# The opening of a retention + ELU kernel: second chunk first, two scalings on another engine, fewer blank products

## The chip, the cores and the metric

The kernel runs on one core of a Trainium2 chip. The metric is the device time of one execution in microseconds (us); the figure for a kernel is the median of several executions. The engines work in parallel, each through its own queue in order, and wait for each other on semaphores: TensorE (PE, with its weight loads PEld), VectorE (DVE), ScalarE (ACT), GpSimd (POOL), and SyncE (SP), whose queue starts all transfers here.

## The reference

Two blocks follow each other. A retention layer, as a recurrence over 768 tokens for 4 batches and 8 heads of 64:

```
for t in range(S):
    state = gamma * state + k[t] (outer) v[t]
    y[t]  = scale * q[t] @ state
```

with gamma = 1 - 2^(-5-h) for head h. Its output, as 3072 tokens of 512 values, goes through two matrix products with an ELU between:

```
h = x @ w_in                       # 512 -> 2048
g = where(h > 0, h, exp(min(h, 0)) - 1)
out = g @ w_out                    # 2048 -> 512
```

Everything is computed in float32. The weights come as 64-bit floats, and the kernel narrows them on the chip.

## The kernel before

The retention works in chunks of 128 tokens; four chunks are a block of 512 tokens (six blocks). For a chunk, the kernel scales v by powers of gamma (`scale_v`), forms scores of q and k within 64-token halves (`score_products`), masks them (`mask_pair`, `scores`), forms the outer products of k and v for the states (`state_products`) and adds them up (`state_sum`). The outputs are sums of two products in PSUM, one within a half (`within`) and one across halves with the state (`across`); VectorE multiplies them by a table of powers (`etab`, built by `powers_of` on ScalarE) into `xb`, the input of the first matrix product. Ahead of the second half of the "across" products, a tiny VectorE copy into `seen` reads PSUM, so that PE waits for the first half.

The weights arrive in sixteen pieces of 1 MB (`wraw`). `prepare` has ScalarE take a piece apart in two or three operations, in one or two halves; with `by_vector` VectorE does the third. `decode` is a generator: each `take()` lets VectorE do the next step, a shift (L191) or a merge (L194, which writes `w_a` or `w_b`), and when a piece is exhausted the next load is issued, which waits until its buffer is free. Pieces 0 and 2 go to `w_a`, pieces 1 and 3 to `w_b`.

The first block's first matrix product is done plainly, in sixteen tiles (`plain_first`); later blocks use Strassen's scheme of seven products. Because only 256 tokens are ready at first, the first five tiles are computed in two halves of columns, and the very first tile begins with a quarter, 128 tokens, as soon as chunk 0 has gone through.

The order of the work is written out by hand: instructions enter each engine's queue in the order in which the program text issues them[...]. The opening (from the function `unread` on) is a list of calls that interleaves chunk 0, chunk 1, the pieces 0 to 2, chunks 2 and 3, and the first five tiles. Two things there feed nothing: `unread(count, n)` multiplies a blank tile into a PSUM bank that nobody reads, and a loop does the same with 28 small blank products ahead of the first scores. They keep PE at work.

The transfers of the opening are issued in this order: chunk 0 in two halves (q and k first), half of piece 0, chunk 1, the other half of piece 0, piece 1, chunk 2, chunk 3, piece 2. The scaling of chunks 0 and 1 runs on VectorE, that of all others on GpSimd (L281):

```
eng = nc.vector if m < 2 else nc.gpsimd
```

Of the kernel before, what the change touches and what calls it, by code (L numbers as in the profile page):

```python
# [18 lines left out]
def kernel(  # L19
# [32 lines left out]
    nc = tc.nc  # L52
# [3 lines left out]
    B, H, S, D, DM, DFF = dims  # L56
    NTOK = B * S
    C = P
    TB = 512
    TH = TB // 2  # L60
# [69 lines left out]
    def load_piece_parts(parts, behind=None):  # L130
        n = len(staged)
        if n < NPIECE:

            t = stage.tile([P, 1024, 2], U32, name="wraw", tag="stage")
            hold(t[:, :, 0].bitcast(FP32), behind)
            staged.append(t)
            for part in range(parts):
                if part:
                    yield
                c = slice(part * 1024 // parts, (part + 1) * 1024 // parts)  # L140
                d = slice(2 * c.start, 2 * c.stop)
                nc.sync.dma_start(t[:, c].rearrange("p c w -> p (c w)"), w_bits[n].bitcast(U32)[:, d])
# [1 line left out]

    def prepare(parts=1, by_vector=False, between=None):

        n = len(prepared)
        if n >= NPIECE:  # L150
            return
        t = staged[n]
        if n < 2 * NQ:
            dst = (w_a, w_b)[n % 2][n // 2].rearrange("p a b c d -> p (a b c d)")
        else:

            dst = w_s[n % NQ].rearrange("p a b c d -> p (a b c d)")[:, 0:1024]
        todo = []
        for part in range(parts):
            if part and between:  # L160
                between()
            c = slice(part * 1024 // parts, (part + 1) * 1024 // parts)
            lo, hi, flat = t[:, c, 0], t[:, c, 1], dst.bitcast(U32)[:, c]
            nc.scalar.activation(flat, lo, AF.Copy, scale=2.0**-29)
            top = dst.bitcast(F8).rearrange("p (c b) -> p c b", b=4)[:, c, 3]
            nc.scalar.activation(top, hi.bitcast(FP32), AF.Copy, scale=2.0**-120, saturate=False)
            if not by_vector:
                nc.scalar.activation(lo.bitcast(FP32), hi.bitcast(FP32), AF.Copy, scale=2.0**-112)
            todo.append((lo, flat, hi if by_vector else None))
        prepared.append((dst, todo))  # L170
# [75 lines left out]
    def powers_of(tokens):  # L246
        for a in range(2):
            for u in range(2):
                nc.scalar.activation(etab[:, a, u, tokens], post[:, tokens], AF.Exp, scale=lny[:, a, u : u + 1])
# [4 lines left out]
    parts = load_piece_parts(2)  # L254
# [17 lines left out]
    carry = [const.tile([P, HP, D], FP32, name=f"carry{n}") for n in range(2)]  # L272
    held = {}

    def scale_v(m):
        if m >= NCHUNK:
            return
        i = chunks[m][1]
        qk, kv = raw[m]
        eng = nc.vector if m < 2 else nc.gpsimd  # L280
        eng.tensor_tensor(  # L281
            out=kv[:, 1], in0=kv[:, 1], in1=vf[:, i].unsqueeze(2).to_broadcast([C, H, D]), op=ALU.mult
        )
# [18 lines left out]
    def score_products(sc, tb, pp, x):  # L302
        qk = raw[tb * CPB + 2 * pp + x][0]
        for p in range(HP):
            for sub in range(2):
                for a in range(2):
                    nc.tensor.matmul(
                        sc[a][rows(sub), x, p, :], lhsT=qk[rows(a), 1, p, rows(sub)],
                        rhs=qk[rows(a), 0, p, rows(sub)], start=True, stop=True, skip_group_check=True,
                    )  # L310
# [13 lines left out]
    def mask_pair(sc, x):  # L324

        place = raw[x][0][:, 1].rearrange("p h c -> p (h c)").rearrange("p (a n t) -> p a n t", a=2, t=D)
        for a in range(2):
            nc.vector.tensor_tensor(
                out=place[:, a], in0=sc[a][:, x], in1=cmask.unsqueeze(1).to_broadcast([P, HP, D]), op=ALU.mult
            )  # L330
# [12 lines left out]
    def state_sum(kvs, tb, pp, x, sub, copy=None):  # L343
        n = 4 * pp + 2 * x + sub
        if fresh(tb, n + 1):
            return
        if fresh(tb, n):
            (copy or nc.scalar.copy)(state(tb, n + 1), kvs[sub][:, x])
        else:
            nc.vector.tensor_tensor(out=state(tb, n + 1), in0=kvs[sub][:, x], in1=state(tb, n), op=ALU.add)  # L350
# [117 lines left out]
    def flush():  # L468
        while later:
            later.pop(0)()  # L470

    def elu(g, h, depth=1, then=None):


        r = epool.tile([P, 512], FP32, name="r", tag="r", bufs=3)
        e = r if len(h.shape) == 2 else r.rearrange("p (a c) -> p a c", c=P)
        nc.scalar.activation(e, h, AF.Relu, scale=-1.0)  # L477
        nc.scalar.activation(e, e, AF.Exp, scale=-1.0)  # L478

        def last():  # L480
            nc.vector.scalar_tensor_tensor(g, e, -1.0, h, ALU.add, ALU.max)  # L481
            if then:
                then()

        while len(later) >= depth:
            later.pop(0)()
        later.append(last)

    def plain_first():

        tiles = [(n, w, row, fi) for n in range(NQ) for w, row in ((w_a, 0), (w_b, 1)) for fi in range(2)]
        banks = []

        def part(k, columns):
            n, w, row, fi = tiles[k]
            for j in range(4):
                nc.tensor.matmul(
                    banks[k][:, columns], lhsT=w[n][:, fi, j // 2, j % 2, :], rhs=xb[:, j, columns],
                    start=(j == 0), stop=(j == 3), skip_group_check=True,
                )  # L500

        for k in range(5):
            hp = bank("aabd"[k]) if k < 4 else ps_r.tile([P, 2, TH], FP32, name="hp", tag="r")
            banks.append(hp.rearrange("p a b -> p (a b)"))
            if k == 0:
                part(0, slice(0, C))
                yield
                part(0, slice(C, 2 * C))
            else:
                part(k, half[0])  # L510
            if k:
                yield
        for k in range(5):
            part(k, half[1])
            n, w, row, fi = tiles[k]
            elu(g_plain[row * NF + 2 * n + fi], banks[k])
            yield
        for k, (n, w, row, fi) in enumerate(tiles[5:]):
            hp = bank("aabd"[k % 4]).rearrange("p a b -> p (a b)")
            for j in range(4):  # L520
                nc.tensor.matmul(  # L521
                    hp, lhsT=w[n][:, fi, j // 2, j % 2, :], rhs=xb[:, j, :], start=(j == 0), stop=(j == 3)
                )
            elu(g_plain[row * NF + 2 * n + fi], hp)
            yield
        flush()
# [158 lines left out]
    def bank(x):  # L685
        return ps_f.tile([P, 2, TH], FP32, name="p" + x, tag=x, bufs=2 if x == "a" else 1)
# [409 lines left out]
    def take(count=1):  # L1096
        for _ in range(count):
            next(piece, None)
# [3 lines left out]
    def unread(count, n):  # L1102
        for _ in range(count):
            nc.tensor.matmul(warm[:, 0:n], lhsT=blank[:, 0:P], rhs=blank[:, 0:n], start=True, stop=True, skip_group_check=True)

    unread(1, TB)
    for n in range(28):
        nc.tensor.matmul(
            (warm, other)[n % 2][rows(n // 2 % 2), 0:D], lhsT=blank[rows(n % 2), 0:D], rhs=blank[rows(n % 2), 0:D],
            start=True, stop=True, skip_group_check=True,  # L1110
        )
# [8 lines left out]
    y = outputs_of_first()  # L1120
    next(y)
    next(y)
    unread(1, TB)
    score_products(sc, 0, 0, 1)
    state_sum(kvs, 0, 0, 0, 1)
    prepare(2, between=lambda: powers_of(slice(2 * C, S)))
    piece = decode(True)
    take()
    take()
    scale_v(1)  # L1130
    mask_pair(sc, 1)
    inner = plain_first()
    next(inner)
    state_products(kvs, 0, 0, 1, range(2))
    state_sum(kvs, 0, 0, 1, 0)
    next(y)
    next(y)
    next(y)
    unread(1, TB)
    next(y, None)  # L1140
    take()
    take()
    take()
    state_sum(kvs, 0, 0, 1, 1)
    scale_v(2)
    scale_v(3)
    prepare(2, by_vector=True)
    next(inner)
    piece = decode()
    take()  # L1150
    take()
    next(inner)
    scores(0, 1)
    states(0, 1)
    take()
    prepare(2)
    piece = decode(True)
    take()
# [26 lines left out]
    for n, _ in enumerate(inner):  # L1185
# [8 lines left out]
        elif n == 10:  # L1194
            scores(1, 0)
            scores(1, 1)
            parts = sums_of_pieces(0)
# [21 lines left out]
    for n in second_of_first():  # L1219
        send_small()  # L1220
        if n == 0:
            run(inputs_of_first(4, [xslot(x) for x in range(3)]))
            parts = sums_of_pieces(2)
# [8 lines left out]
        elif n == 2:  # L1232
            next_piece()
            parts = sums_of_pieces(4)
# [5 lines left out]
        elif n == 4:  # L1240
            run(inputs_of_first(6, [hslot(), hslot(), xslot(0)]))
            decode_all()
            parts = sums_of_pieces(6)
# [85 lines left out]
    for tb in range(2, NTB):  # L1329
# [24 lines left out]
        tail, parts = iter(()), combine_x_parts()  # L1354
# [122 lines left out]
```

## Time and profile before

| what | us |
|---|---|
| median of three executions | 635.99 |
| lowest, highest | 635.6, 638.48 |
| the profiled execution, its own time | 636.29 |
| span of its profile | 634.4 |
| PE busy in the span | 626.7 |
| PE busy in 0 to 7.9 / 7.9 to 30.6 | 6.45 / 20.91 |
| start of the second column half of the first tile (pa L497) | 30.56 |

The span is the time from the first to the last instruction in the profile; times in the timeline count from its start. A timeline row gives start and length in us, the engine, the line, the operation, what it writes and reads, shapes and the number of merged instructions; in brackets stands how long the engine was idle before and who released it. A float32 product on PE is recorded as two passes, so four products of 128x256 show as eight. The records of consecutive instructions overlap a little, so that a stretch of equal instructions is shorter than their lengths added up.

### The profile page before, as it was taken

How to read it: one execution, taken by the hardware profiler on the slowest of the kernel's cores; microseconds unless marked ns; L12 is line 12 of the kernel's file. 1: busy time of each engine (PE TensorE's matmuls, PEld its weight loads, DVE VectorE, ACT ScalarE, POOL GpSimd, SP SyncE). 2: the span in 40 equal slices, each digit the busy share in tenths (PEclk: the TensorE clock that was granted, in tenths of full speed). 3: DMA queues.
4: the chain of work that ended last, by engine and by line, in shares of the span. 5: the costliest groups of instructions: out<-in, count | busy, mean ns of one | idle time of the engine just before them, and what ended most of it. 6: DMA issues, size and time to landing. Idle time of an engine off the chain costs nothing.

```text
span 634.4 us, 16149 instructions
## 1 busy us (share of the span) xinstructions
PE 626.7 (99%) x6680; PEld 560.7 (88%) x6680; DVE 481.7 (76%) x870; ACT 252.9 (40%) x472; POOL 40.6 (6%) x40
## 2 busy tenths in 40 slices
PE   8999999999999999999999999999999999999998
PEld 5764568888899999889999989999988999988997
DVE  5779979978879685589676598867489878558975
ACT  6599635014551113554112556111465311366311
POOL 1111000003600000200000100000110000000000
PEclk9999999999999999999999999999999999999999
DMA  8698867687477778504889701789820697700794
GB/s 336 264 390 307 269 205 222 189 248 258 176 239 228 242 254 272 239 2 135 277 267 312 290 4 55 258 283 286 302 100 4 218 299 236 238 24 2 231 309 158
DMA packets 75897, 136.85 MB, mean 216 GB/s; under 512 B 6320, under 2 KB 31792, under 8 KB 70704
## 3 DMA queue, kind: packets, MB, share of 16 engines
q1 hardware_dynamic: 75824, 135.82, 64.2%
q8 instruction: 53, 0.87, 0.5%
q14 instruction: 20, 0.16, 0.1%
HBM read 114.56 MB, written 21.23 MB: 214 GB/s over the span
## 4 chain that ended last, share of the span: by engine, by line
PE 94%; DVE 4%; issue 1%; ACT 0%; DVEq 0%
PE pa L953 20%; PE pa L911 10%; PE pd L953 10%; PE pb L953 5%; PE pa L865 5%; PE pb L911 4%; PE pa L521 3%; PE qa L911 3%; PE x L611 3%; PE pa L740 2%; PE pd L865 2%; PE qd L911 2%; PE pd L911 2%; PE pa L611 2%; PE y L394 2%; PE kv L338 2%
## 5 line engine op out<-in xcount | busy, mean ns | idle before, releaser
L961 ACT COPY ms<-pa 128x128 f32<-128x128 f32 x104 | 27.6, 265 | 147.1 <-PE pa L953 143.7
L953 PE MATMUL pa<-ts,wq 128*128 128x128 f32 x560 | 74.2, 275 | 0.0
L953 PE MATMUL pd<-ts,wq 128*128 128x128 f32 x552 | 73.6, 276 | 0.1
L953 PEld LDWEIGHTS pa<-ts,wq 128*128 128x128 f32 x560 | 68.5, 192 | 0.4
L953 PEld LDWEIGHTS pd<-ts,wq 128*128 128x128 f32 x552 | 67.1, 192 | 0.9 <-DVE res L965 0.5
L953 PE MATMUL pa<-gC,wq 128*128 128x128 f32 x480 | 64.6, 278 | 0.0
L478 ACT ACTIVATE r<-r 128x512 f32<-128x512 f32 x96 | 60.5, 631 | 3.0
L953 PEld LDWEIGHTS pa<-gC,wq 128*128 128x128 f32 x480 | 59.0, 192 | 1.3
L477 ACT ACTIVATE r<-gC 128x512 f32<-128x512 f32 x64 | 39.9, 624 | 32.0 <-DVE gC L919 32.0
L965 DVE TENSOR_TENSOR res<-pd,ms 128x128 f32<-128x128 f32 x68 | 19.4, 286 | 39.6 <-PE pd L953 38.4
L281 POOL TENSOR_TENSOR chunk<-chunk,vf 128x512 f32<-128x512 f32 x22 | 26.3, 1199 | 318.4 <-DMA chunk<-in_qkv_dram 153.5
L481 DVE SCALAR_TENSOR_TENSOR gC<-r,gC 128x512 f32<-128x512 f32 x64 | 44.3, 724 | 0.7 <-ACT r L478 0.7
L827 DVE TENSOR_TENSOR ts<-gC,ts 128x512 f32<-128x512 f32 x60 | 41.3, 688 | 1.0
L827 DVE TENSOR_TENSOR ts<-gC 128x512 f32<-128x512 f32 x60 | 40.9, 682 | 0.0
L953 PE MATMUL pb<-gC,wq 128*128 128x128 f32 x240 | 31.7, 275 | 0.0
L986 ACT COPY res<-pa 128x128 f32<-128x128 f32 x34 | 9.0, 265 | 55.1 <-PE pa L953 55.1
L953 PEld LDWEIGHTS pb<-gC,wq 128*128 128x128 f32 x240 | 29.2, 192 | 0.0
L690 ACT COPY m<-pa 128x512 f32<-128x512 f32 x24 | 13.9, 581 | 30.1 <-PE pa L911 14.2
L919 DVE TENSOR_TENSOR gC<-qa,gC 128x512 f32<-128x512 f32 x8 | 5.5, 692 | 25.1 <-PE qa L911 18.3
L911 PE MATMUL pa<-xt,w_s 128*128 128x256 f32 x96 | 23.0, 382 | 0.0
L911 PE MATMUL pa<-xt,w_b 128*128 128x256 f32 x96 | 23.0, 382 | 0.0
L965 DVE TENSOR_TENSOR res<-res 128x512 f32<-128x512 f32 (+1 forms) x31 | 20.6, 666 | 3.0 <-DVE res L965 0.5
(256 smaller groups left out, 1258.4 us busy)
## 6 DMA issues: line engine op xcount, KB each, us to landing
wq<-scratch_dram SPq DMA_DIRECT2D x277, 256.0 KB, 4.2
chunk<-in_qkv_dram SPq DMA_DIRECT2D x23, 1024.0 KB, 8.3
wraw<-in_w_dram SPq DMA_DIRECT2D x15, 1024.0 KB, 6.1
out_dram<-res SPq DMA_DIRECT2D x14, 256.0 KB, 3.8
scratch_dram<-gT SPq DMA_DIRECT2D x12, 256.0 KB, 4.2
scratch_dram<-m SPq DMA_DIRECT2D x12, 192.0 KB, 5.6
scratch_dram<-so SPq DMA_DIRECT2D x4, 512.0 KB, 4.8
scratch_dram<-wi SPq DMA_DIRECT2D x2, 1024.0 KB, 5.1
```

Of the source, the lines that this page charges most:

```text
L281: eng.tensor_tensor(out=kv[:, 1], in0=kv[:, 1], in1=vf[:, i].unsqueeze(2).to_broadcast([C, H, D]), op=ALU.mult)
L477: nc.scalar.activation(e, h, AF.Relu, scale=-1.0)
L478: nc.scalar.activation(e, e, AF.Exp, scale=-1.0)
L481: nc.vector.scalar_tensor_tensor(g, e, -1.0, h, ALU.add, ALU.max)
L521: nc.tensor.matmul(hp, lhsT=w[n][:, fi, j // 2, j % 2, :], rhs=xb[:, j, :], start=(j == 0), stop=(j == 3))
L611: nc.tensor.matmul(X[j][:, d, :], lhsT=w[j][:, d * P : d * P + P], rhs=x[j], start=(n == 0 and d == 0), stop=at_end, skip_group_check=True,)
L827: sub = lambda o, x, y: nc.vector.tensor_tensor(out=o, in0=x, in1=y, op=ALU.subtract)
L865: nc.tensor.matmul(ps[:, f, :], lhsT=lhs[f], rhs=xs[j][k], start=(begin and f == 0), stop=True, skip_group_check=True,)
L911: nc.tensor.matmul(ps[:, fi, :], lhsT=w[:, fi, j2, :], rhs=x[:, j2, :], start=(j in (1, 7) and fi == 0 and j2 == 0), stop=(j2 == 1), skip_ ...
L953: nc.tensor.matmul(ps, lhsT=w[:, f, :], rhs=ts[j][k][:, f, :], start=(begin and f == 0), stop=(f == 3), skip_group_check=True,)
L961: nc.scalar.copy(m, ps)
L965: nc.vector.tensor_tensor(out=o, in0=x, in1=y, op=ALU.add)
```

## The change

The second chunk's score products, scaling, masks, state products and outputs come directly behind the first chunk's, and the first decode steps and the first quarter tile follow behind or between them. The powers for the tokens from 256 on are built behind piece 1's preparation, where they had stood between the halves of piece 0 (so `prepare` loses its `between`). The scaling of chunks 2 and 3 goes from GpSimd to VectorE, behind the decode of piece 1. The fourth tile's first half is itself split into two quarters, with the scores and states of chunks 2 and 3 between them. Of the blank products, 20 small ones remain of 28; the large one ahead of chunk 1's scores has 256 columns in place of 512; the one behind chunk 1's outputs is gone.

```diff
-    def prepare(parts=1, by_vector=False, between=None):
+    def prepare(parts=1, by_vector=False):
...
-            if part and between:
-                between()
...
-    def scale_v(m):
+    def scale_v(m, by_vector=False):
...
-        eng = nc.vector if m < 2 else nc.gpsimd
+        eng = nc.vector if by_vector or m < 2 else nc.gpsimd
...
                 part(0, slice(C, 2 * C))
+            elif k == 3:
+                part(k, slice(0, C))
+                yield
+                part(k, slice(C, 2 * C))
             else:
                 part(k, half[0])
...
-    for n in range(28):
+    for n in range(20):
...
     next(y)
     next(y)
-    unread(1, TB)
+    unread(1, TH)
     score_products(sc, 0, 0, 1)
     state_sum(kvs, 0, 0, 0, 1)
-    prepare(2, between=lambda: powers_of(slice(2 * C, S)))
+    prepare(2)
     piece = decode(True)
-    take()
-    take()
     scale_v(1)
     mask_pair(sc, 1)
-    inner = plain_first()
-    next(inner)
     state_products(kvs, 0, 0, 1, range(2))
     state_sum(kvs, 0, 0, 1, 0)
     next(y)
+    take()
     next(y)
+    take()
     next(y)
-    unread(1, TB)
+    inner = plain_first()
+    next(inner)
     next(y, None)
     take()
     take()
     take()
     state_sum(kvs, 0, 0, 1, 1)
-    scale_v(2)
-    scale_v(3)
     prepare(2, by_vector=True)
+    powers_of(slice(2 * C, S))
     next(inner)
     piece = decode()
     take()
     take()
+    take()
+    scale_v(2, True)
+    scale_v(3, True)
+    next(inner)
     next(inner)
     scores(0, 1)
     states(0, 1)
-    take()
     prepare(2)
     piece = decode(True)
     take()
```

## The prediction

> **What bounds the kernel now.** I read the page's shares and slices first, then the busy time in three stretches, then the timeline of each engine over the first 35 us, then the waits.
>
> ```profile
> PE 626.7 (99%) x6680; PEld 560.7 (88%) x6680; DVE 481.7 (76%) x870; ACT 252.9 (40%) x472; POOL 40.6 (6%) x40
> PE   8999999999999999999999999999999999999998
> ```
>
> TensorE is busy nearly everywhere. The stretches (PE busy is the second figure, then PEld, DVE, ACT, POOL) show where it is not:
>
> ```profile
> 0.00:7.90 7.90, 6.45 (x120) 4.18 (x124) 3.75 (x26) 3.23 (x6) 1.56 (x8) 1.00 0.78 255
> 7.90:30.60 22.70, 20.91 (x501) 16.19 (x494) 16.96 (x38) 16.38 (x23) 2.31 (x3) 1.00 0.82 330
> 30.60:634.40 603.80, 599.38 (x6073) 540.31 (x6071) 461.03 (x807) 233.27 (x443) 36.69 (x29) 1.00 0.64 211
> ```
>
> From 30.6 us on PE misses 4.4 us of 604 us: it sets the end, so the kernel ends earlier by what this stage starts earlier. The stage begins with the second halves of the first five products (pa L497 at 30.56). All that the change touches lies before it, where blank products, waits and real work alternate. The timeline there (start, length, then idle time before and its releaser):
>
> ```profile
> 5.00 1.08 PE L307 MATMUL sc<-chunk 64*64 64x64 f32 x32
> 10.81 0.69 PE L307 MATMUL sc<-chunk 64*64 64x64 f32 x32
> 11.83 1.13 PE L497 MATMUL pa<-xb,w_a 128*128 128x128 f32 x8 [0.33 <-DVE w_a L194]
> 16.16 3.11 PE L497 MATMUL pa<-xb,w_a 128*128 128x128 f32 x16
> 19.79 1.99 PE L497 MATMUL pb<-xb,w_b 128*128 128x256 f32 x8 [0.52 <-DVE w_b L194]
> 25.66 1.36 PE L394 MATMUL y<-chunk 64*64 64x64 f32 x63
> 27.81 0.69 PE L409 MATMUL y<-chunk 64*64 64x64 f32 x32 [0.26 <-DVE seen L378]
> 28.50 2.22 PE L497 MATMUL hp<-xb,w_a 128*128 128x256 f32 x8
> 30.56 3.62 PE L497 MATMUL pa<-xb,w_a 128*128 128x256 f32 x16
> ```
> ```profile
> 18.43 1.31 DVE L194 CUSTOM_DVE_ANT_0 w_b<-wraw,w_b 128x1024 uint16<-128x1024 uint16 x1
> 20.67 1.31 DVE L194 CUSTOM_DVE_ANT_0 w_b<-wraw,w_b 128x1024 uint16<-128x1024 uint16 x1
> 27.51 0.25 DVE L378 COPY seen<-y 128x8 f32<-128x8 f32 x2 [1.18 <-PE y L409]
> 28.57 1.29 DVE L384 TENSOR_TENSOR xb<-y,etab 128x512 f32<-128x512 f32 x2 [0.22 <-PE y L409]
> 18.12 1.07 POOL L281 TENSOR_TENSOR chunk<-chunk,vf 128x512 f32<-128x512 f32 x1 [3.05 <-DMA chunk<-in_qkv_dram]
> 20.37 1.06 POOL L281 TENSOR_TENSOR chunk<-chunk,vf 128x512 f32<-128x512 f32 x1 [1.18 <-DMA chunk<-in_qkv_dram]
> 22.86 0.69 ACT L164 ACTIVATE w_a<-wraw 128x512 uint32<-128x512 uint32 x1 [5.17 <-DMA wraw<-in_w_dram]
> 24.24 0.65 ACT L168 ACTIVATE wraw<-wraw 128x512 f32<-128x512 f32 x1
> 32.48 0.60 ACT L477 ACTIVATE r<-pa 128x512 f32<-128x512 f32 x1 [2.26 <-PE pa L497]
> ```
>
> The order to follow is y L394, seen L378, second half of y L409, hp, pa. ScalarE waited 2.26 us for PE at 32.48; VectorE's chain through the four merges (L194) of pieces 0 and 1 decides when PE gets to y.
>
> [...] there is a slow start: the 32 score passes took 1.08 us at 5.00 and 0.69 at 10.81. [...] the two w_b merges, begun inside the two GpSimd scalings, took 1.31 us, the other merges of this shape 0.68 to 0.69. [...]
>
> **The change, part by part.** Prices are from the timeline: a 128x256 pass 0.216 us, so four products (eight passes) 1.73 and with 128 columns 0.86; VectorE start to start 0.60 for a scaling, 0.34 for a sum, 0.45 + 0.60 for a shift and its merge.
>
> *Eight blank products fewer.* 56 passes filled 3.45 to about 5.0, so eight products are 0.43 us. The first chunk's q and k land at about 4.7 (issue at 0.74 plus 4.0, the shortest landing that the transfers show), so the scores start about 0.15 earlier, not 0.43. This 0.15 is lost again at the second chunk, which lands at about 10.5 by the transfer records.
>
> *Blank product before the second scores halved, a later one removed.* 0.43 and 0.86 us of PE. The scores of chunk 1 go from 10.80 to about 10.6, bound by the landing.
>
> *Chunk 1 first.* The shift and merge of piece 0's first half (L191 10.54, L194 10.99 to 11.68) and the first product (PE 11.83 to 12.89) no longer stand before chunk 1's scaling, masks and state products. New VectorE starts: scaling 10.57, masks 11.33 (scores end at 11.29), state sum 12.03, shift 12.37, the two "seen" copies 12.92, merge 13.08 to 13.77, xb 13.75 and 14.09, shift 14.43 (ScalarE is done with that half at 14.41, as before), merge 14.89 to 15.58, sum 15.49, then piece 1: 15.83, 16.28, merge 16.73 to 17.42. Before, piece 1's first merge ended at 19.74.
>
> *Scaling of chunks 2 and 3 to VectorE.* Adds 2 x 0.68 us to VectorE, removes 2.13 us of GpSimd and with it 2 x 0.62 us of blocked merge. Piece 1's second merge ends at 18.92 (before: 21.98). Then chunk 2's scaling 18.83, chunk 3's waits for its landing until 20.37 and ends at 21.05. Queued behind it stand the masks L318 and the state sums; PE waits for these, but chunk 3's scores are not done before 21.2, so this wait costs nothing. Without that cover it would cost up to 1 us.
>
> *Powers of the last tokens (4 x 0.64 = 2.55 us of ScalarE) moved behind piece 1.* Before they filled 9.92 to 12.47, ahead of a piece half that lands only about then. Now they fill 17.7 to 20.2, in the 5.17 us that ScalarE idles before 22.86. First use is L384, later than 26. Cost nothing; 2.55 us of ScalarE were the cover gone.
>
> *Fourth product split.* Its first 128 columns (0.86) before the scores of chunks 2 and 3, the rest behind their state products. The passes sum to the same; up to 0.2 for extra changes of shape.
>
> PE then: first product 13.92 and 14.78, second 15.73 (its weights: 15.58 + 0.15), third 17.57, fourth's first half 19.30, scores 20.2 to 21.25, states 22.2, fourth's rest to 23.1, y L394 at 23.1 (before 25.66). By the old distance (25.66 to 27.51) "seen" would come at 24.95. It can't: in VectorE's queue the shift of piece 2's first half stands ahead of it, and that needs ScalarE, which ends at 24.24 + 0.65 = 24.89 on a piece that lands at 22.8. No load ahead of that one is issued differently: SP's first eight issues keep their order and waits, and what comes free earlier (buffers of pieces 0 and 1) queues behind transfers that run anyway. So the shift starts at 24.93 and "seen" at 25.28. From there the old distances hold: y's second half +0.30, pa L497 +3.05, so pa at 28.33 instead of 30.56. **Gain: 27.51 - 25.28 = 2.23 us.** PE has about 0.3 us to spare against that floor.
>
> Behind it, ScalarE is free at 30.2 (third operation on piece 3, 29.09 + 1.14), and the first elu needs pa's product at about 30.2: 2.26 us earlier, just enough. The load of piece 5 waits on piece 2's last merge and moves from 30.92 to about 28.7, behind transfers that end by 28.1. The later loads follow their merges.
>
> The profiled execution had 636.29 us, 634.4 of span and 1.9 around it. Minus 2.2 it gives 634.1; it stood 0.3 above the median of 635.99, so I predict **633.8 us**.
>
> **Rivals.** (1) *Part only.* If the w_b merges are slow for another reason than GpSimd, they end 0.6 and 1.2 us later, the fourth product's first half starts at 20.55, y L394 at 24.4, "seen" at 26.2: gain 1.3, 634.7 us. The same follows if PE's small products take longer than their old distances. For it: only 0.3 us spare. Against: both long merges, and only these, lie on GpSimd operations.
> (2) *Swallowed.* ScalarE is 92 to 98% busy from 33 to 63; if it can't start earlier, PE runs into full PSUM banks and the gain is 0, 636.0. Against: its 2.26 us of waiting at 32.48, and one wait of 4.5 us for PE in the stretch to 80.
> (3) *Slower.* Less blank work leaves PE idle for some 0.4 us around 4.6 and more later[...]. Passes at half rate cost as much again: 0.39 for scores of a chunk, about as much for its states, 0.5 + 0.4 for its y, 0.86 for each 128-column quarter of the first product; from 7.9 to about 15 us that is some 3 us. [...] when the full rate comes only after the first product, at about 16, the gain is used up, and beyond, to about 20, it is 638. [...] Against: PE stays busy from 13.9 on and has no gap over 0.5 us before.
> (4) *More.* Piece 2's landing is a floor for everything here; over 2.5 us would need a stall behind 30.6 to vanish too: 633.0.
>
> **How the numbers follow.** Full gain (2.0 to 2.5) 0.58, part (0.6 to 2.0) 0.24, swallowed 0.07, slower 0.05, more 0.06. The likeliest gives 633.5 to 634.0. Parts and repetitions (635.6 to 636.3 but for one of 638.48) stretch the range to 632.8 to 636.0. A half per cent (3.2 us), about what a measurement of this kernel can tell from no change, is below 632.8 or above 639.2: faster 0.06, slower 0.03, same 0.91.
>
> **What would show it.** Right: sc of chunk 1 near 10.6; first product near 13.9; w_b merges of 0.69; pb L497 near 17.6; ScalarE still at 22.86; "seen" of y near 25.3, pa's second half near 28.3, first elu near 30.2, the rest shifted by the same 2.2. Wrong: score passes over 1 us at 10.6 (clock), an idle wait for chunk 3 that ends behind its scores, "seen" released by PE later than 25.5, or waits of PE for gC after 40 us.

## The result: slower by 0.4%

The changed kernel took 639.27 us in the median (637.21 to 642.23, 20 executions); the kernel before, beside it, 636.45 (635.25 to 639.21). The ratio is 1.0042, with a 95% interval of 1.003 to 1.0055: 2.7 us slower. The prediction was 633.8 us, a gain of 2.2, with a range that ended at 636.0: the change goes the other way. The profiled execution took 637.8 us with a span of 635.7, near the low end of the twenty, so the profile can account for about half of the loss only; the other half is taken up below.

The page of the changed kernel, its shares, slices and a queue of transfers that the page calls "instruction" (packets, MB, share of the transfer engines):

```profile
PE 624.2 (98%) x6670; PEld 560.0 (88%) x6670; DVE 482.1 (76%) x872; ACT 252.8 (40%) x472; POOL 37.6 (6%) x38
PE   7899999999999999999999999999999999999998
q8 instruction: 53, 0.87, 0.5%
```

The busy time in the same three stretches as before, the second one now ending where the second half of the first tile starts (31.8 instead of 30.6):

```profile
0.00:7.90 7.90, 6.01 (x136) 3.80 (x140) 3.92 (x27) 3.23 (x6) 1.56 (x8) 1.00 0.80 254
7.90:31.80 23.90, 18.67 (x479) 15.79 (x470) 16.49 (x40) 16.38 (x23) 0.17 (x1) 1.00 0.76 314
31.80:635.70 603.90, 599.49 (x6073) 540.43 (x6071) 461.64 (x807) 233.18 (x443) 35.88 (x29) 1.00 0.64 211
```

PE is busy for 2.24 us less in the second stretch than before (18.67 against 20.91; 1.3 of it is blank work taken out), and yet the stretch is 1.2 us longer: PE stands still there for 5.23 us instead of 1.79. The third stretch is as long as before, 603.9 against 603.8. So in the profile the whole difference is made in the opening. PE's timeline there:

```profile
10.62 0.69 PE L305 MATMUL sc<-chunk 64*64 64x64 f32 x32 [0.61 <-DMA chunk<-in_qkv_dram]
11.34 0.69 PE L336 MATMUL kv<-chunk 64*64 64x64 f32 x32
13.27 0.27 PE L392 MATMUL pb<-chunk 64*64 64x64 f32 x2 [1.16 <-issue]
15.20 3.77 PE L495 MATMUL pa<-xb,w_a 128*128 128x128 f32 x24 [0.23 <-DVE w_a L192]
18.96 1.97 PE L495 MATMUL pb<-xb,w_b 128*128 128x256 f32 x8
20.76 1.05 PE L495 MATMUL pd<-xb,w_b 128*128 128x128 f32 x8
21.75 1.16 PE L305 MATMUL sc<-chunk 64*64 64x64 f32 x64
23.77 1.16 PE L495 MATMUL pd<-xb,w_b 128*128 128x128 f32 x8
24.86 0.46 PE L392 MATMUL y<-chunk 64*64 64x64 f32 x15
27.56 0.93 PE L392 MATMUL y<-chunk 64*64 64x64 f32 x49 [2.25 <-issue]
29.29 0.69 PE L407 MATMUL y<-chunk 64*64 64x64 f32 x32 [0.33 <-DVE seen L376]
29.98 1.97 PE L495 MATMUL hp<-xb,w_a 128*128 128x256 f32 x8
31.78 2.54 PE L495 MATMUL pa<-xb,w_a 128*128 128x256 f32 x11
```

VectorE and ScalarE in the same window:

```profile
18.12 0.69 DVE L192 CUSTOM_DVE_ANT_0 w_b<-wraw,w_b 128x1024 uint16<-128x1024 uint16 x1
19.76 0.69 DVE L192 CUSTOM_DVE_ANT_0 w_b<-wraw,w_b 128x1024 uint16<-128x1024 uint16 x1
28.99 0.24 DVE L376 COPY seen<-y 128x8 f32<-128x8 f32 x2 [2.64 <-PE y L407]
22.88 0.69 ACT L162 ACTIVATE w_a<-wraw 128x512 uint32<-128x512 uint32 x1 [2.54 <-DMA wraw<-in_w_dram]
33.70 0.60 ACT L475 ACTIVATE r<-pa 128x512 f32<-128x512 f32 x1 [3.50 <-PE pa L495]
```

(The functions stand two lines higher than before: L192 is L194 of before, L392 is L394, L495 is L497.) The scores of the second chunk start where they were forecast, both merges into `w_b` take 0.69 instead of 1.31, ScalarE starts piece 2 where it did. The two lines to look at are those with "issue": in the middle of a run of equal small products, after 1 and after 15 of them, PE stops for 1.16 and for 2.25 us. Nothing releases it, neither VectorE nor a transfer of data. The waits of PE say the same (idle us, how often, the longest):

```profile
PE y L392 <- issue: 2.2, 1, 2.2
PE pb L392 <- issue: 1.2, 1, 1.2
```

In the kernel before, the same view has no line with "issue"; its largest waits are 1.5 us for a blank tile and 1.2 us in two parts for `h`.

### What PE waits for

Queue 8 above, by its name, brings instructions: 53 packets in 0.87 MB are 16.4 KB each. 6670 passes and as many weight loads over 53 packets are 252 records per packet, 126 passes each. That the packets are PE's is inferred, from this number and from the times below; what one packet brings is called a block from here on. One of them is under way during the second stall; the transfers in 25.2 to 26.5 us, by queue:

```profile
q1 hardware_dynamic: 42, 0.25, 47.5%
q8 instruction: 1, 0.02, 5.3%
```

By the trace's transfer records, that one packet is under way from 25.26 to 26.36, and PE goes on at 27.56, 1.2 us after its end. The packet of the first stall runs from 10.98 to 11.93, and PE goes on at 13.27, 1.3 after. So in both stalls a block took 1 us of transfer, and PE went on some 1.2 us after that (1.2 to 1.6 over all stalls in the openings of the runs below). Where PE runs dry in this way, it has done the same number of recorded passes in every trace: 222 or 223, 477 or 478, 605; with 126 passes to a block, one more would end near 350, which is an estimate from these counts. The same is seen far behind the opening: in four kernels of 6662 to 6672 passes (`b20`, `b20long`, `a20wide` and `a20nosplit` below) PE stands still after 1998 passes, for 0.58 to 1.53 us, and in three of them after 3504 or 3505, for 1.20 to 1.54 us. The kernel before has its first four blocks at 9.74, 15.86, 23.38 and 27.53 and hardly notices: its third packet ends at 24.45, so by the same 1.2 us PE would go on from it at about 25.65 (an estimate), and until 25.66 PE was at work on the fourth product, eight passes of 0.216 us. Only behind the fourth block is it slower, by about 0.2 us at `hp`, whose eight passes take 2.22 us there and 1.97 in the change.

My theory from this, for the experiments to test ("fetch" in what was expected of them): which instruction is the last of a block depends only on how many stand before it. Where a block ends among products of 128x256, PE has 0.216 us of work per pass in hand and the fetch is hidden; where it ends in a run of 64x64 products, which follow each other about every 0.015 us in the profile of the change, PE runs dry unless the block was asked for early. The change moved the block ends in the work (18 passes fewer in front by the blank products, 16 of them by the small ones, and 8 more by the split) and put small products where large ones were. The rival theory is the clock: with less blank work, so with less time in the blank products rather than a smaller number of them, PE may stay for longer at the slow rate of its start (in the kernel before, 32 score passes took 1.08 us at 5.00 and 0.69 at 10.81).

### The profile page after: what moved, and what is told of

Same layout as the page of the kernel before. It is cut to its first block, busy times and chain, and to the rows that moved or that the text cites. A ratio compares the mean times of both kernels' runs of the same rounds, so it can differ in the third digit from the quotient of the medians.

```text
span 635.7 us, 16127 instructions
## 1 busy us (share of the span) xinstructions
PE 624.2 (98%) x6670; PEld 560.0 (88%) x6670; DVE 482.1 (76%) x872; ACT 252.8 (40%) x472; POOL 37.6 (6%) x38
## 4 chain that ended last, share of the span: by engine, by line
PE 91%; DVE 4%; ACT 2%; issue 1%; DMA 1%; SPq 0%
PE pa L955 20%; PE pa L913 10%; PE pd L955 10%; PE pb L955 5%; PE pa L867 5%; PE pb L913 4%; PE qa L913 3%; PE x L613 3%; PE pa L742 2%; PE pa L523 2%; PE pd L867 2%; PE qd L913 2%; PE pd L913 2%; PE pa L613 2%; PE y L392 2%; PE kv L336 2%
## 5 line engine op out<-in xcount | busy, mean ns | idle before, releaser
L279 POOL TENSOR_TENSOR chunk<-chunk,vf 128x512 f32<-128x512 f32 x20 | 23.4, 1173 | 322.3 <-PE pa L867 228.1
L913 PE MATMUL pa<-xb,w_a 128*128 128x256 f32 x96 | 22.7, 379 | 0.0
```

Of the source, the lines that this page charges most:

```text
L279: eng.tensor_tensor(out=kv[:, 1], in0=kv[:, 1], in1=vf[:, i].unsqueeze(2).to_broadcast([C, H, D]), op=ALU.mult)
L913: nc.tensor.matmul(ps[:, fi, :], lhsT=w[:, fi, j2, :], rhs=x[:, j2, :], start=(j in (1, 7) and fi == 0 and j2 == 0), stop=(j2 == 1), skip_ ...
```

## The experiments

All times are medians; "ratio" is to the kernel before, measured beside the run. The blank products feed nothing, so where an edit alters them all outputs are still computed in full.

### The number of blank products alone

`b20` is the kernel before with the smaller number, and nothing else of the change:

```diff
-    for n in range(28):
+    for n in range(20):
```

> The kernel before with 20 small blank products instead of 28, nothing else. Two theories for the changed kernel's loss. Fetch: PE's instructions come in blocks of 16 KB (about 127 recorded passes); where a block ends inside a run of small 64x64 passes, PE runs dry for up to 2.3 us, and the number of instructions issued earlier decides where the blocks end. [...] Fetch expects the block ends at 16 passes further on in the work (from the 5th to the 21st pass of y, out of the first tile's second weight load): 0 to 1 us slower, 636.5 to 637.5. Clock expects most of the loss here: 638 to 639, score passes of chunk 1 over 0.7 us in part of the executions.

Measured: 640.42 us, ratio 1.0055 (1.0031 to 1.008), more than either theory had expected. The one number by itself costs the kernel before about as much as the whole change does (1.0042; the intervals overlap). Its profile is the slowest of its twelve executions (645.41), so its length is not typical, but it shows two ways in which time goes:

```profile
12.64 1.13 PE L307 MATMUL sc<-chunk 64*64 64x64 f32 x32
28.46 0.57 PE L394 MATMUL y<-chunk 64*64 64x64 f32 x22
30.52 0.85 PE L394 MATMUL y<-chunk 64*64 64x64 f32 x41 [1.49 <-issue]
```

The scores of chunk 1, 0.69 in both kernels, take 1.13: here, by the trace's clock records, the full rate came only at 14.2 us, where in the kernel before it is there from 7.8 on. This is the case of my third rival, and in this profile it is not small: the third product starts at 22.59, 2.8 us later than before, ahead of any long stall. And the third block ends 22 passes into y, where in the kernel before it ends 6 passes in, for a stall of 1.5. (The opening's slow rate does not appear in the column of the granted clock, which has 1.00 from 5 us on in this run, nor in its mean, since the records begin with the first full rate; the durations show it.) So this run does not separate count and time; `b20long` below does.

`a28` is the changed kernel with the old number:

```diff
-    for n in range(20):
+    for n in range(28):
```

> The changed kernel with 28 small blank products again. Fetch expects the block ends 16 passes earlier in the work: the 2.2 us stall in the outputs of chunks 2 and 3 moves to the fourth product's second half, where queued 128-column passes cover part of it, the 1.2 us stall moves from chunk 1's outputs into its state products: 635 to 638. Clock expects as much as 28 blanks give, 636 to 637.5. Without either the forecast of 633.8 holds.

Measured: 638.46 us, ratio 1.0024 (1.0012 to 1.0036), span 635.9. By the medians less slow than the change (the intervals overlap), but slower than either theory had expected. The stalls are not gone; they have moved, as PE's waits show:

```profile
PE y L407 <- issue: 1.2, 1, 1.2
PE pd L495 <- issue: 1.0, 1, 1.0
PE kv L336 <- issue: 0.8, 1, 0.8
```

The sixteen passes more in front bring the first block's end back into the state products of chunk 1 (`kv`), the third's to the last pass of the fourth product (`pd`), the fourth's to the last pass of the second half of y. The second half of pa starts at 31.39.

`a20wide` gives back blank time without the count, with one blank tile of 128 columns behind the loop:

```diff
         ...
+    unread(1, P)
```

> The changed kernel with one blank product of 128 columns behind the 20 small ones: about the time of the eight removed ones (0.43 us at half rate), but 2 passes instead of 16. Clock expects it to be as fast as the changed kernel with 28. Fetch expects the block ends within 2 passes of the changed kernel's and so the same stalls: 638.5 to 640.

Measured: 640.35 us, ratio 1.0049 (1.003 to 1.0068). The time given back brings nothing that can be seen: the stalls stand nearly where they stood, now two passes earlier for the two that were added:

```profile
24.98 0.45 PE L392 MATMUL y<-chunk 64*64 64x64 f32 x13
27.45 1.29 PE L392 MATMUL y<-chunk 64*64 64x64 f32 x50 [2.02 <-issue]
```

The piece of y behind the stall takes 1.29 us for 50 passes where the change takes 0.93 for 49. PE in three windows of this run (length, PE, PEld, DVE, ACT and POOL busy, granted clock, transfers):

```profile
24.90:28.30 3.40, 1.38 (x60) 1.17 (x62) 1.51 (x4) 3.34 (x5) 0.00 (x0) 0.94 0.26 101
28.30:31.70 3.40, 3.14 (x85) 2.78 (x78) 1.48 (x4) 1.62 (x2) 0.00 (x0) 0.55 0.02 5
32.00:36.00 4.00, 4.00 (x20) 3.52 (x19) 1.47 (x3) 1.06 (x2) 0.00 (x0) 1.00 0.37 84
```

The window with the stall, in which PE is busy for 1.38 of 3.40 us, is followed by one of 3.4 us at about half rate, and then full rate again. The trace's clock records have half rate from 27.92 to 31.33 us, so for 3.41 us, beginning 0.47 us behind the stall of 2.02 us. A stall of about this length does not always have such a window behind it: behind the change's 2.25 us, and behind 1.73 us in `a20nosplit`, the profiles show full rate.

A window of this length lowers the mean granted clock of an execution by half of 3.41 in 636, to 0.997. Of the changed kernel's twenty executions four have a mean of 1.0 and a median of 637.5, ten have 0.997 and 639.25, five 0.995 and 641.1, one 0.992 and 639.7: in the first three groups about 1.8 us from one to the next, near half of 3.41; that each step is one such window is an estimate from these figures. Of the kernel before, in the four comparisons of the runs below, 48 of 49, 42 of 44, 33 of 35 and 23 of 27 executions have 0.999 or more. The lower mean does not always cost that: in `a28` above the six executions at 0.997 have the median of the eleven at 1.0 (638.2 and 638.3). So the change's +2.7 are some 1.3 in the opening and, most likely, one or two half-rate windows in most executions. That these windows come from the stalls is argued, not shown: in two of the three profiles that hold such windows (this one and `b20long`) the window begins right behind a stall, in the third (`a28nosplit_more`) behind other idle time, and the profile of the change itself has none.

### Count against time of the blanks

Three runs hold the blank time near one kernel's and the count at another's. `a28short`: the change with 28 blanks of 44 columns, near 20 of 64 in time. `b36short`: before with 36 of 50, near 28 of 64. `b20long`: before with 20 of 90, near 28 of 64. The edit has one form, here with `a28short`'s numbers:

```diff
-    for n in range(20):
+    for n in range(28):
         nc.tensor.matmul(
-            (warm, other)[n % 2][rows(n // 2 % 2), 0:D], lhsT=blank[rows(n % 2), 0:D], rhs=blank[rows(n % 2), 0:D],
+            (warm, other)[n % 2][rows(n // 2 % 2), 0:44], lhsT=blank[rows(n % 2), 0:D], rhs=blank[rows(n % 2), 0:44],
```

> The changed kernel with 28 blank products of 44 columns: the number of instructions of 28, about the time of 20. Fetch expects it as fast as the changed kernel with 28 full ones. Clock expects no gain against the changed kernel: 638.5 to 640.

Measured: 638.6 us, ratio 1.0031 (1.0012 to 1.005): between `a28` (1.0024) and the change (1.0042), so the time alone does not say which of them it goes with. The places do: its stalls end at 25.44 and 29.17, near `a28`'s 25.41 and 29.41. Shorter blanks of the same number leave the stalls where they are.

> The kernel before with 36 blank products of 50 columns instead of 28 of 64: the same blank time, 16 passes more, no other change. In all five traces so far PE ran dry at the same counts, 223 (or 224), 477 (or 478) and 605 recorded passes, until 1.2 us after a 16 KB instruction block had arrived. Fetch expects these block ends 16 passes earlier in the work, the one at 605 in the middle of y's second half with no long passes queued: a stall of 1 us or more there, 637.5 to 639. Clock expects no change: 636 to 637.

Measured: 640.59 us, ratio 1.0048 (1.0023 to 1.0073). Slower, and by more than the count theory had expected, but not where I expected it: the opening hardly moves (second half of pa at 30.88, before 30.56), since the block that I had put into y was asked for early. The stall stands far behind, ahead of the first large products of a later stage:

```profile
223.66 0.38 PE L953 MATMUL pa<-gC,wq 128*128 128x128 f32 x1
225.26 1.05 PE L953 MATMUL pa<-gC,wq 128*128 128x128 f32 x7 [1.22 <-issue]
```

> The kernel before with 20 blank products of 90 columns: the blank time of 28, 16 passes fewer. It parts the loss of 20 plain ones (ratio 1.0055) in two. Clock expects no loss: 636 to 637, full rate from about 7.8 us. Fetch expects the loss to stay: 638 to 640, with a stall of 1.5 us or more at pass 478.

Measured: 639.05 us, ratio 1.0049 (1.0028 to 1.007). Again slower with the blank time kept, with full rate from 6.9 us on; so what its profile loses goes with the count, not with late full rate. Again my place was wrong: the opening is as before (pa at 30.37), since the block at y was asked for at 23.46. What is lost is lost behind it, for instance in the state products of the second block:

```profile
65.35 1.08 PE L338 MATMUL kv<-chunk 64*64 64x64 f32 x45
68.09 2.05 PE L338 MATMUL kv<-chunk 64*64 64x64 f32 x67 [1.66 <-issue]
```

with, right behind it, a window at half rate between two at full rate (same columns as above):

```profile
60.00:66.00 6.00, 6.00 (x170) 3.74 (x163) 5.20 (x8) 5.44 (x7) 0.68 (x1) 1.00 1.02 334
69.00:72.00 3.00, 3.00 (x46) 1.94 (x40) 2.88 (x6) 1.77 (x3) 0.00 (x0) 0.54 0.55 110
```

From the start of the third stage to the end the profiled execution, the slowest of eight, takes 610.27 us, before 603.88. Four stalls there, of 1.66, 0.93, 0.62 and 1.54 us, and half of one window of 3.41 make 6.5, against a difference of 6.4. (For the stall of 0.62 the profile names a VectorE copy, but it too ends 1.3 us behind the arrival of a block.) So eight products fewer at the start went with stalls of up to 1.66 us far behind the opening, the three longest in runs of small products (`kv` and `y`). Both misses have one reason. When a block was asked for did not follow from the count alone: for the third block the request came 12 to 30 passes ahead of the place where PE needs it in most profiles, 55 to 126 ahead in three (`b20long` and `b36short` among them), and without a lead, at 25.26, in the change. What sets the lead (the state of PE's queue, its waits on semaphores, other transfers) these runs do not tell apart.

### The other parts

`bvec`: the kernel before with the scaling of chunks 2 and 3 on VectorE behind piece 1, PE's instructions unchanged:

```diff
+    def scale_v(m, by_vector=False):
+        eng = nc.vector if by_vector or m < 2 else nc.gpsimd
...
-    scale_v(2)
-    scale_v(3)
     prepare(2, by_vector=True)
...
     take()
     take()
+    take()
+    scale_v(2, True)
+    scale_v(3, True)
     next(inner)
     scores(0, 1)
     states(0, 1)
-    take()
```

> The kernel before with the scaling of chunks 2 and 3 on VectorE behind piece 1, and nothing else: PE's instructions are the same, one for one. My forecast priced this part at 2 x 0.62 us of merges no longer blocked by GpSimd; on PE's path that is the first merge: 0.6 us earlier at the third product. Without a fetch effect: 635.8 to 636.1. Fetch: the block at 478 may be asked for earlier too, or not; between 635.5 and 637.

Measured: 636.23 us, ratio 0.9996 (0.9984 to 1.0007), span 633.8. The opening gains: the third product starts at 18.63 instead of 19.79, the second half of pa at 29.45 instead of 30.56. Of these 1.1 us 0.6 are left in the span, and 0.3 in the median, which can't be told from nothing.

`a28nosplit`: the change with 28 blanks and the fourth product in one piece, as before:

```diff
-            elif k == 3:
-                part(k, slice(0, C))
-                yield
-                part(k, slice(C, 2 * C))
...
-    for n in range(20):
+    for n in range(28):
...
     scale_v(3, True)
     next(inner)
-    next(inner)
```

> The changed kernel with 28 blank products and the fourth product whole again, between the states and outputs of chunks 2 and 3 as in the kernel before: behind the first three products PE's stream is the old one, so the block ends at 477 and 605 fall where they fell before, with long passes queued ahead. What remains of the change is chunk 1 first (with the stall of about 1 us at pass 223) and the scaling on VectorE. Fetch expects 635 to 636.5, less than the changed kernel with 28 (638.5) by 2. If the stalls at 477 and 605 stay above 1 us, or the time stays at 638, the place of the blocks is not what decides.

Measured: 635.94 us, ratio 0.9986 (0.997 to 1.0001), span 632.2, a profiled execution of 634.29. PE's timeline:

```profile
22.24 1.99 PE L495 MATMUL pd<-xb,w_b 128*128 128x256 f32 x8
24.16 0.34 PE L392 MATMUL y<-chunk 64*64 64x64 f32 x7
24.70 1.05 PE L392 MATMUL y<-chunk 64*64 64x64 f32 x57 [0.20 <-issue]
29.04 3.62 PE L495 MATMUL pa<-xb,w_a 128*128 128x256 f32 x16
```

The block ends 7 passes into y, and costs 0.20 instead of 2.25: the whole product of eight passes stands in front of it. The stall at the first block is 0.42. pa starts at 29.04, 2.74 us ahead of the change and 1.52 ahead of before; 0.69 more is gained behind it.

`a20nosplit`: the same with 20 blanks, so the change with only the split undone.

```diff
-    for n in range(28):
+    for n in range(20):
```

> The same kernel (28 blanks, fourth product whole, ratio 0.9986) with 20 blanks: the fourth corner of the square of 28 or 20 blanks and whole or split. Fetch expects the block ends 16 passes further on, in y of chunk 1, in the 22nd pass of y of chunks 2 and 3, and at other places behind 60 us: 2 to 4 us slower, 638.5 to 640.5. If blanks and split had costs of their own that add, this kernel would stand at 0.9986 plus the 0.0018 between 28 and 20 with the split: 637.1.

Measured: 641.52 us, ratio 1.0082 (1.0061 to 1.0102, four executions), the slowest of all, and 1 us above what I had expected. The block at 477 stalls PE again, for 1.73 us until 27.62; the full rate comes only at 14.2, and the third product starts at 19.48, with 28 blanks at 18.32; later stalls stand at 68, 208 and 326 us. The four corners are 1.0024 (28, split), 0.9986 (28, whole), 1.0042 (20, split) and 1.0082 (20, whole): undoing the split helps with 28 blanks and hurts with 20. The two edits do not add up, as they would if each had a price of its own. The block ends, which the sum of both moves, behave like this; but the late full rate came in this corner alone, and its 1.2 us at the third product are not the block ends' doing.

`a28pool`: `a28nosplit` with the scaling left on GpSimd, at its old place.

```diff
+    scale_v(2)
+    scale_v(3)
     prepare(2, by_vector=True)
...
-    scale_v(2, True)
-    scale_v(3, True)
```

> The kernel with 28 blanks and the fourth product whole (ratio 0.9986), but with the scaling of chunks 2 and 3 on GpSimd as before: PE's instructions are the same, so what is left of the change is chunk 1 first and the later powers. My forecast's price of the scaling: both merges of piece 1 at 1.31 us again, PE's third product 0.6 us later than with VectorE, so about 0.6 us slower than that kernel: 636 to 637. If the merges were slow for another reason they stay at 0.69.

Measured: 636.42 us, ratio 0.9994 (0.9979 to 1.0009), span 633.1. I expected both merges at 1.31; they took 0.70 and 0.69. Another step was long, as the timeline shows:

```profile
18.24 1.10 POOL L279 TENSOR_TENSOR chunk<-chunk,vf 128x512 f32<-128x512 f32 x1 [3.11 <-DMA chunk<-in_qkv_dram]
18.35 1.28 DVE L188 TENSOR_SCALAR wraw<-wraw 128x512 f32<-128x512 f32 x1
```

VectorE's first step on the second half of piece 1 (L188, a multiplication, ahead of the shift), begun 0.11 us behind GpSimd's scaling, takes 1.28 instead of 0.42 (`a28nosplit`) and ends 0.29 after it. The third product still starts only 0.3 us later than without (18.59 against 18.32). So the move of the scaling to VectorE is worth a few tenths here; in either pair of runs that is less than the medians can tell apart.

`a28nosplit_more` repeats `a28nosplit`, with no edit.

> The kernel with 28 blanks and the fourth product whole again, unchanged, for a narrower interval: 0.9986, between 0.997 and 1.000; its profile again about 2 us under that of the kernel before where no half-rate window falls into it.

Measured: 636.72 us, ratio 1.0 (0.9979 to 1.002), span 634.6. Taken together the two measurements of this kernel show no gain over the kernel before. Of its 14 executions 5 have a mean clock below 0.9985 (the expectation of the next run says 6), though they are no slower than the rest. Its profile is one of these: 6.8 us at half rate, behind PE's idle time from 9.6 to 10.7, ahead of chunk 1's scores (two windows, columns as above):

```profile
11.50:18.00 6.50, 6.17 (x109) 5.65 (x110) 4.91 (x14) 4.72 (x8) 0.17 (x1) 0.50 1.01 423
19.00:25.00 6.00, 6.00 (x147) 5.21 (x146) 4.42 (x10) 3.52 (x7) 0.00 (x0) 1.00 1.01 419
```

That idle time is where the change halved the large blank product. `a28blanks` puts its full width back, and the removed one too:

```diff
-    unread(1, TH)
+    unread(1, TB)
...
     next(y)
+    unread(1, TB)
     inner = plain_first()
     next(inner)
```

> The kernel with 28 blanks and the fourth product whole, and both large blank products as before the change: of the change remain chunk 1 first, the later powers and the scaling on VectorE. Two passes more than without the third blank product, as many as in the kernel before. Clock: PE idles less around 10 and 14 us, so half-rate windows become rarer; they stood in 6 of 14 executions of the kernel without these blanks when it was repeated. Fetch: the block end at 223 as with 28 blanks, the later ones exactly as before the change. The blanks themselves cost up to 0.3 us each on PE's path. Forecast: 0.998 of the time before, 0.9965 to 0.9995; if the blanks' cost outweighs the windows, 1.000.

Measured: 635.57 us (634.66 to 637.7, 22 executions), ratio 0.9973 (0.9959 to 0.9987), span 632.5. 2 of 22 executions are below 0.9985. This version, second chunk first, scaling on VectorE, all blank work as before and the fourth product whole, beats both kernels, the one before by 0.27% or 1.7 us (0.13 to 0.41%). Its waits on "issue" come to 0.5 us, once, in `kv`. That the blank products themselves, and not a luckier place of the blocks, make the difference to `a28nosplit` is not shown: they add two passes, and the two intervals overlap.

## Why the prediction was wrong

By its own steps, forecast and measured start in us:

| step | forecast | measured | late by |
|---|---|---|---|
| scores of chunk 1 | 10.6 | 10.62 | 0.0 |
| first product | 13.92 | 15.20 | 1.3 |
| third product | 17.57 | 18.96 | 1.4 |
| scores of 2 and 3 | 20.2 | 21.75 | 1.55 |
| y, first half | 23.1 | 24.86 | 1.8 |
| "seen" | 25.28 | 28.99 | 3.7 |
| second half of pa | 28.33 | 31.78 | 3.45 |

The delay comes in at two places. *Chunk 1 first* held up to the state products (11.34) and then lost 1.16 us to the first block's end, a wait that the forecast did not have. The small distances on the way to y add 0.5, of which the split has 0.2, as allowed for. Then *"From there the old distances hold"* failed outright: from y to "seen" PE was taken to run as before, and stood 2.25 us still in between. The sum fits: 1.3 + 0.5 + 2.25 less the 0.33 us that PE had to spare against the floor of piece 2 is 3.7, and hp and pa then took 0.26 less than before. Two entries of *The change, part by part* went wrong, since I had costed them in time alone: *Eight blank products fewer* as 0.43 us of PE that nothing needs, *Fourth product split* as up to 0.2. What they do besides is move the block ends: 16 passes fewer in front, 8 more ahead of y, and half as much long work ahead of y. With both undone (`a28nosplit`) the two stalls shrink from 1.16 and 2.25 us to 0.42 and 0.20; with one of them undone (`a28`, `a20nosplit`) stalls of 1.0 us and more remain. Rival 1 came closest in words ("PE's small products take longer than their old distances"), but with a price of 0.9 us and still faster than before.

What was right: both `w_b` merges fell to 0.69; ScalarE's start at 22.88; the powers of the last tokens cost nothing behind piece 1; no wait for chunk 3's scaling. Behind the second half of pa the rest took 603.9 us, before 603.9, so everything was shifted by what the opening did, as the forecast said, only in the other direction. With the two stalls taken down to 0.42 and 0.20 (`a28nosplit`), the span is 632.2, which is the forecast's 634.4 less 2.2; but only 1.52 of it comes from the opening, so the agreement is partly chance.

Rival 3, slower by the clock, named a real effect: late full rate was seen in the profiles of `b20` and `a20nosplit`, both with 20 blanks (at 14.2 us, before at 7.8). In the profile of the change it was not: the clock is full from 6.0 us on. Whether other executions of the change had it late can't be told, since the mean clock does not count it. What the mean clock does show is 0.992 to 0.997 in 16 of 20 executions, so time at a lower rate, by the groups above the likely reason why the median lost twice what the profile did. Not settled: why the third block was asked for without a lead in the change, and whether and which of its stalls bring the windows.

## What to carry to other kernels

Before an edit that only adds or removes small instructions ahead of a tuned stage, look in the profile for PE waits on "issue", and ask what work PE has where its instruction blocks end: in the change PE stood still for 2.25 us in a run of 128 small passes, from the start of the transfer to 1.2 us behind its end; with eight passes of 256 columns ahead of the run it stood for 0.20 us (`a28nosplit`) or not at all (the kernel before). An edit's price is then not only its time but, as in `b20long`, also its count, and it can show hundreds of microseconds later (at 208, 225 and 328 us here); test such an edit with its count restored and its time kept, and the other way round. Read the mean granted clock of all executions, not only of the profiled one: a profile near the fastest execution can hide a loss that most of them have.

## What the runs showed of the hardware

- A packet of 16.4 KB in the queue named "instruction" (one for about 126 recorded passes of PE) took 0.9 to 1.1 us in the openings of both kernels, and where PE ran dry it went on 1.2 to 1.6 us after the packet's end. In runs of 64x64 products PE was idle for 1.16 and 2.25 us in the change, with no semaphore in sight.
- Eight tiny products fewer, which feed nothing, made the kernel before 0.55% slower (0.31 to 0.8%); with the time of the eight given back to the other 20 it was still 0.49% (0.28 to 0.7%).
- Stalls of 1.66 us (`b20long`) and 2.02 us (`a20wide`) were followed by 3.41 us at half rate, stalls of 1.73 us (`a20nosplit`) and 2.25 us (the change) were not; in the changed kernel a mean clock of 0.997 in place of 1.0 went with about 1.8 us of time, in `a28` with none.
- A VectorE multiplication begun 0.11 us behind GpSimd's scaling took 1.28 us instead of 0.42 (`a28pool`, `a28nosplit`), the two merges begun inside GpSimd's scalings 1.31 instead of 0.69 (the kernel before, the change).
